# Seeding PSUM from ScalarE in a weight split, and a new order for the first ten units

## Chip, cores and metric

The kernel runs on one core of one Trainium2 chip. The metric is device microseconds of one execution; lower is better. Shown are the median of several runs and one profiled execution, whose span the trace covers instruction by instruction.

## What is computed

Three layers in fp32, on 3072 tokens (4 batches of 768), 8 heads of 48, so 384 features.

```python
for t in range(S):
    cur = einsum('bhd,bhe->bhde', u * k[t], v[t])
    y[t] = einsum('bhd,bhde->bhe', r[t], state + cur)
    state = w[t][..., None] * state + einsum('bhd,bhe->bhde', k[t], v[t])
...
h = x @ moe_w_in                       # 384 -> 1024
sm = softmax(h)
solu = h * sm
ln = (solu - mean(solu)) / sqrt(var(solu) + 1e-6) * g_ln
x = ln @ moe_w_out                     # 1024 -> 384
...
h = x @ moe2_w_in                      # 384 -> 2048
out = maximum(0.01 * h, h) @ moe2_w_out
```

The weights arrive as 64-bit floats. The kernel decodes them on the chip from pairs of 32-bit words into a high part and a low part (both fp32r, the form that TensorE multiplies in one pass), and computes each product as high by high, high by low and low by high.

## The kernel before

The tokens form 24 units of 128 rows (`NU`). A unit goes through the attention part (`prep…`, `att_…`), then `x_t`, `x_hi`, `x_lo` (turn it and split it), `mm1` (the 1024-wide product, 18 matmuls in two halves), the softmax steps (`soft_max`, `soft_e`, `soft_z`, `soft_nm`, `soft_c`, `soft_q`), `z_t`, `z_hi`, `z_lo` (turn and split again), and, three units at a time, `mm2` (the product with the output weights). The last layer (`mm3`, `g_…`, `mm4`) follows for the whole batch of tokens and fills more than half of the time with matmuls.

Nothing schedules itself: the order of work is three tables of step names, `FIRST` (units 0 to 9), `LOOP` (units 10 to 13) and `LAST`. Each entry calls a function, and each function appends its instructions to the queues of the engines, each of which runs its own queue strictly in that order. `warm` and `warm_k` are matmuls of constants whose result nobody reads.

The weights of the first layers are decoded in 14 slices, in the steps `w1_a` (ScalarE), `w1_e`, `w1_f`, `w1_h`, `w1_b` (VectorE), `w1_c` (split, ScalarE and TensorE) and `w1_d` (ScalarE). The first six slices ("i") are of `w_in`, 512 columns each; the other eight ("o") are of `w_out`, 384 columns each, and are multiplied by `g_ln` on the way. After `w1_b` the value stands as a tile `t` (the top of the number) and a negated rest in the low part's home (`w1ol` for "o"). `w1_c` must form t minus the negated rest minus the high part in PSUM (`PO`), for `w1_d` to copy out as the final low part. `ident` is an identity matrix in fp32, `minus` its negative in fp32r.

Of the kernel before, what the change touches and what calls it, by code (L numbers as in the profile page):

```python
# [43 lines left out]
0; att_mid 0; warm 13; w1_c; att_mul_next 0; prep_vd 0; w1_b; w1_d; att_y 0; att_state 0; prep4 1; load_g; att_x 0;
att_u 1; att_mid 1; w1_c; w1_b; prep_bonus 1; load_tr 2; w1_a; att_mul_next 1; prep_diag 1; load_tr 3; w1_d; prep1
2; att_scores 1; w1_e; x_t 0; load_nat 2; att_evac_s 1; load_o 1; prep2 2; w1_a; w1_c; x_hi 0; prep_vd 1; att_state
1; x_lm 0; x_lo 0; prep_k 2; w1_d; mm1 0 0; w1_f; att_kt 2; w1_a; prep3 2; mm1 0 1; prep_p 1; prep1 3; prep_check 2;
att_evac_k 2; prep_check 3; prep4 2; soft_max 0; att_y 1; prep_k 3; att_u 2; w1_a; w1_h; prep_p 2; att_x 1; att_mid
2; soft_e 0; warm_k 12; att_kt 3; warm_k 8; x_t 1; prep_bonus 2; att_scores 2; w1_e; att_evac_k 3; load_tr 4; soft_z
0; w1_g; w1_b; x_hi 1; prep_diag 2; prep_state 2; w1_f; x_lm 1; prep2 3; w1_c; att_evac_s 2; prep3 3; soft_nm 0;  # L50
x_lo 1; soft_c 0; mm1 1 0; w1_e; prep_p 3; prep_check 4; w1_h; w1_a; w1_f; w1_e; w1_h; prep_state 3; w1_b; w1_f;
w1_d; att_mul_next 2; z_t 0; prep4 3; w1_h; soft_q 0; load_nat 3; mm1 1 1; prep1 4; prep_vd 2; z_hi 0 0; z_lm 0 0;
w1_c; z_hi 0 1; prep_p 4; w1_b; z_lm 0 1; prep_k 4; z_lo 0 0; load_nat 4; att_scores 3; prep_bonus 3; z_lo 0 1;
w1_d; att_y 2; soft_max 1; att_x 2; w1_c; soft_e 1; w1_e; x_t 2; att_state 2; att_kt 4; x_hi 2; w1_a; soft_z 1;
prep_state 4; w1_f; prep2 4; soft_nm 1; w1_b; w1_h; w1_d; att_u 3; x_lm 2; w1_b; x_lo 2; w1_a; prep3 4; soft_c 1;
mm1 2 0; z_t 1; att_mid 3; w1_c; prep_diag 3; z_hi 1 0; load_tr 5; z_hi 1 1; att_mul_next 3; load_nat 5; z_lm 1 0;
att_evac_k 4; w1_e; att_state 3; att_evac_s 3; z_lm 1 1; w1_f; z_lo 1 0; prep1 5; prep_vd 3; mm1 2 1; w1_d; prep4 4;
att_u 4; z_lo 1 1; soft_q 1; att_y 3; soft_max 2; att_x 3; w1_h; prep_k 5; w1_c; att_mid 4; soft_e 2; prep_bonus 4;
x_t 3; w1_d; soft_z 2; w1_b; x_hi 3; att_kt 5; att_scores 4; prep_p 5; w1_e; x_lm 3; w1_c; prep_diag 4; w1_f; w1_a;
prep2 5; w1_e; x_lo 3; mm1 3 0; w1_h; soft_nm 2; prep_state 5; att_mul_next 4; att_evac_k 5; w1_b; w1_f; load_tr 6;  # L60
prep3 5; soft_c 2; w1_h; z_t 2; prep1 6; w1_d; prep_k 6; w1_c; z_hi 2 0; z_lm 2 0; prep_vd 4; mm1 3 1; z_hi 2 1;
w1_d; w1_b; z_lm 2 1; z_lo 2 0; att_state 4; att_evac_s 4; w1_c; soft_max 3; soft_q 2; z_lo 2 1; soft_e 3; att_y 4;
w1_d; att_u 5; prep4 5; att_x 4; soft_z 3; prep_check 5; att_scores 5; att_kt 6; prep_p 6; soft_nm 3; load_nat 6;
x_t 4; prep_bonus 5; prep2 6; x_hi 4; mm2a 4; soft_c 3; prep_check 6; soft_q 3; x_lo 4; load_tr 7; mm1 4 0; prep3 6;
prep4 6; prep_state 6; prep_bonus 6; z_t 3; z_hi 3 0; z_hi 3 1; att_mid 5; mm1 4 1; prep_diag 5; load_tr 8;
att_evac_k 6; z_lm 3 0; prep_vd 5; prep1 7; prep2 7; att_mul_next 5; att_evac_s 5; z_lo 3 0; z_lm 3 1; load_nat 7;
mm2b 4; att_scores 6; prep_p 7; soft_max 4; z_lo 3 1; mm2_out 4; prep_diag 6; att_state 5; prep3 7; att_y 5; att_u
6; prep_state 7; soft_e 4; mm2a 5; prep_check 7; att_x 5; soft_z 4; prep_k 7; prep4 7; x_t 5; mm2b 5; x_hi 5; x_lo
5; mm1 5 0; att_kt 7; soft_nm 4; prep_bonus 7; prep1 8; att_mid 6; soft_c 4; att_evac_s 6; att_mul_next 6; soft_q 4;
prep_vd 6; att_state 6; prep_k 8; mm2_out 5; z_t 4; prep_check 8; z_hi 4 0; z_hi 4 1; z_lo 4 0; z_lo 4 1; load_nat  # L70
8; prep2 8; mm1 5 1; att_evac_k 7; prep_diag 7; att_y 6; att_u 7; att_scores 7; soft_max 5; mm2a 6; att_x 6; att_kt
8; soft_e 5; prep_bonus 8; prep_p 8; x_t 6; att_mid 7; soft_z 5; soft_nm 5; prep3 8; prep_state 8; x_hi 6; prep_diag
8; soft_c 5; load_nat 9; load_tr 9; prep4 8; mm2b 6; x_lo 6; z_t 5; load_tr 10; prep_vd 7; att_mul_next 7; z_hi 5 0;
att_evac_s 7; z_hi 5 1; prep_bonus 9; att_state 7; prep_check 9; mm1 6 0; mm2_out 6; prep1 9; z_lo 5 0; att_evac_k
8; z_lo 5 1; prep_diag 9; mm1 6 1; soft_max 6; att_y 7; att_x 7; att_u 8; prep_p 9; soft_q 5; att_scores 8; prep1
10; soft_e 6; soft_z 6; mm2a 7; prep2 9; prep3 9; prep_vd 8; att_mid 8; att_mul_next 8; x_t 7; soft_nm 6; prep_k 9;
prep_k 10; mm2b 7; x_hi 7; x_lo 7; prep2 10; att_state 8; soft_c 6; mm1 7 0; z_t 6; mm2_out 7; att_evac_s 8; prep4
9; z_hi 6 0; prep_p 10; load_nat 10; z_hi 6 1; z_lo 6 0; mm1 7 1; att_kt 9; prep_state 9; z_lo 6 1; load_tr 11;
soft_max 7; soft_q 6; att_y 8; prep_vd 9; att_scores 9; prep_bonus 10; att_evac_k 9; att_u 9; att_x 8; soft_e 7;
att_kt 10; att_mid 9; soft_z 7; x_t 8; x_hi 8; soft_nm 7; att_mul_next 9; att_evac_s 9; att_evac_k 10; load_nat 11;  # L80
mm2a 8; x_lo 8; mm1 8 0; prep3 10; soft_c 7; z_t 7; prep1 11; prep_k 11; prep_diag 10; z_hi 7 0; prep_check 10; z_lo
7 0; att_state 9; soft_q 7; z_hi 7 1; prep_p 11; prep4 10; mm1 8 1; mm2b 8; prep_state 10; prep2 11; prep3 11;
prep_bonus 11; mm2_out 8; load_tr 12; z_lo 7 1; att_u 10; att_scores 10; prep_vd 10; soft_max 8; att_y 9; soft_e 8;
mm2a 9; att_x 9; prep_check 11; prep_state 11; x_t 9; mm2b 9; prep4 11; soft_z 8; att_mid 10; att_mul_next 10; x_hi
9; x_lo 9; prep1 12; soft_nm 8; prep_diag 11; soft_c 8; soft_q 8; att_evac_s 10; mm1 9 0; z_t 8; z_hi 8 0; prep_vd
11; load_tr 13; load_nat 12; mm2_out 9; mm1 9 1; prep_bonus 12; z_lo 8 0; prep_k 12; prep_p 12; att_state 10; z_hi 8
1; z_lo 8 1; prep2 12; prep_check 12; att_kt 11; att_evac_k 11
# [1086 lines left out]
```

## Time and profile before

| | |
|---|---|
| median of 3 runs | 740.12 us (739.97 to 740.4) |
| the profiled execution | 740.35 us, its span 738.6 us |
| TensorE, matmul | 721.6 us busy (98%) |
| VectorE | 502.4 us busy (68%) |
| ScalarE | 362.3 us busy (49%) |
| GpSimd | 193.9 us busy (26%) |

The shares are over the whole span, and the stages differ. In the first 340 us all the engines work on the attention part and the first layers; after that the time is almost only matmuls of the last layer. TensorE's records overlap, since a matmul is recorded until its last column has left the array: what one costs in a row of others is the distance between two starts, not its recorded length. For the other engines two records that follow each other without a wait overlap by some hundredths of a microsecond too.

### The profile page before, as it was taken

To read this page: it belongs to the slowest core of one execution; us is meant where nothing else is said; L and a number is where in the kernel's file an instruction comes from. 1 tells how busy PE (TensorE), PEld (TensorE's weight loads), DVE (VectorE), ACT (ScalarE), POOL (GpSimd) and SP (SyncE) were. 2 spreads that over 40 slices of the span, in tenths; PEclk is the share of its full clock that TensorE was granted. 3 is DMA by queue.
4 is the path that set the end of the run, shared out by engine and by line. 5 is a ranking of instruction groups with operands and counts; after the bars stand their busy time and mean duration, and the time that the engine had idled before them with its cause. 6 is when DMAs were issued, how large, how long until landed. Compare 5 with 4: busy or idle time off the path is not lost.

```text
span 738.6 us, 15199 instructions
## 1 busy us (share of the span) xinstructions
PE 721.6 (98%) x6243; PEld 607.4 (82%) x6243; DVE 502.4 (68%) x877; ACT 362.3 (49%) x668; POOL 193.9 (26%) x261
## 2 busy tenths in 40 slices
...
GB/s 327 280 168 109 130 149 115 140 151 102 184 149 166 117 110 77 79 120 159 190 130 86 43 65 1 92 80 0 1 86 0 1 12 32 1 1 43 1 0 47
DMA packets 30753, 69.10 MB, mean 94 GB/s; under 512 B 3260, under 2 KB 15956, under 8 KB 30548
## 3 DMA queue, kind: packets, MB, share of 16 engines
...
## 4 chain that ended last, share of the span: by engine, by line


## 5 line engine op out<-in xcount | busy, mean ns | idle before, releaser
L987 DVE TENSOR_TENSOR gw<-t,gh 128x512 fp32r<-128x512 f32 x96 | 68.2, 712 | 53.3 <-ACT gh L983 53.1
L983 ACT CAST gh<-t 128x512 fp32r<-128x512 f32 x96 | 59.2, 620 | 72.5 <-DVE t L979 58.3
L953 POOL TENSOR_TENSOR x2l<-x2l,x2h 128x1536 fp32r<-128x1536 f32 x4 | 14.1, 3514 | 276.8 <-ACT x2h L949 276.8
L979 DVE TENSOR_TENSOR t<-t,PZ 128x512 f32<-128x512 f32 x48 | 32.9, 686 | 68.7 <-ACT t L975 68.7
L979 DVE TENSOR_TENSOR t<-t,PK 128x512 f32<-128x512 f32 x48 | 32.9, 686 | 58.7 <-ACT t L975 58.7
L975 ACT ACTIVATE t<-PK 128x512 f32<-128x512 f32 x48 | 28.6, 596 | 73.8 <-PE PK L967 70.3
L975 ACT ACTIVATE t<-PZ 128x512 f32<-128x512 f32 x48 | 28.6, 596 | 71.8 <-PE PZ L967 71.0
L764 PE MATMUL PO<-zh,w1oh 128*128 128x384 f32 x168 | 59.9, 356 | 0.0
L708 PE MATMUL PH<-w1ih,xh 128*128 128x512 f32 x144 | 58.4, 405 | 0.1
L708 PE MATMUL PH<-w1ih,xl 128*128 128x512 f32 x144 | 57.0, 396 | 0.2
L708 PE MATMUL PH<-w1il,xh 128*128 128x512 f32 x144 | 56.4, 392 | 0.0
L764 PE MATMUL PO<-zh,w1ol 128*128 128x384 f32 x168 | 56.4, 336 | 0.0
L764 PE MATMUL PO<-zl,w1oh 128*128 128x384 f32 x168 | 56.3, 335 | 0.0
L967 PE MATMUL PK<-x2h,w2ih 128*128 128x512 f32 x144 | 56.2, 391 | 0.0
L967 PE MATMUL PZ<-x2h,w2ih 128*128 128x512 f32 x144 | 56.1, 390 | 0.0
L967 PE MATMUL PZ<-x2h,w2il 128*128 128x512 f32 x144 | 56.1, 389 | 0.0
L967 PE MATMUL PZ<-x2l,w2ih 128*128 128x512 f32 x144 | 56.1, 389 | 0.0
L967 PE MATMUL PK<-x2l,w2ih 128*128 128x512 f32 x144 | 56.0, 389 | 0.0
L967 PE MATMUL PK<-x2h,w2il 128*128 128x512 f32 x144 | 56.0, 389 | 0.0
L560 POOL TENSOR_TENSOR vd<-natv,dg 64x192 f32<-64x192 f32 (+1 forms) x57 | 36.5, 640 | 10.7 <-DVE dg L549 8.0
L997 PE MATMUL PH<-gw,w2oh 128*128 128x512 f32 x96 | 37.5, 390 | 0.5 <-DVE gw L987 0.5
L997 PE MATMUL PA<-gw,w2oh 128*128 128x512 f32 x96 | 37.4, 389 | 0.0
...
## 6 DMA issues: line engine op xcount, KB each, us to landing
...
```

Of the source, the lines that this page charges most:

```text
L560: pool.tensor_tensor(out=d[p:p + (64 if h else 128), h:h + 4], in0=nats[i][0][a, h:h + 4], in1=dgs[i][a, h:h + 4].to_broadcast([a.stop - a ...
L708: pe.matmul(out=PH[:, half], lhsT=a[:, kc], rhs=c[:, kc, 512 * half:512 * half + 512], start=(n == 0), stop=(n == 8))
L764: pe.matmul(out=o2[m], lhsT=a[:, c, 128 * m:128 * m + 128], rhs=d[:, c], start=(c == 0 and q == 0), stop=(c == K1 - 1 and q == 2))
L953: (dve if g < 2 else pool).tensor_tensor(out=xl, in0=f(xl), in1=f(xh), op=ALU.subtract)
L967: pe.matmul(out=h_at[n % 2], lhsT=a[:, kc, 128 * o:128 * o + 128], rhs=d[:, kc], start=(q == 0), stop=(q == 8))
L975: act.activation(out=gs[n][0], in_=h_at[n % 2], func=AF.Copy, scale=0.01)
L979: dve.tensor_tensor(out=t, in0=t, in1=h_at[n % 2], op=ALU.max)
L983: act.copy(out=gh, in_=t)
L987: dve.tensor_tensor(out=gw, in0=t, in1=f(gh), op=ALU.subtract)
L997: pe.matmul(out=at, lhsT=a[:, c % 4, 128 * o:128 * o + 128], rhs=d[:, a0:b0], start=(c == 0 and q == 0), stop=(c == K2 - 1 and q == 2 and ...
```

## The change

For the eight "o" slices, `w1_c` no longer scales `t` in place and copies it into PSUM by an identity product. ScalarE writes the scaled `t` straight into `PO`, makes the high part from `PO`, and TensorE only adds the two negative products onto what stands there. The six "i" slices stay as they were. The lines below are moved by four by the change (L856 of before is L860 for the "i" slices; for "o" the scaling is L854, the high part L855, the two products L856 and L857).

```diff
             key, t = w1_done.pop(0)
             hi, lo = w1_home(key)
+            d = PO[:, 0:t.shape[1]]
             if key[0] == "o":
-                act.activation(out=t, in_=t, func=AF.Copy, scale=gl[:, key[1]:key[1] + 1])
-            act.copy(out=hi, in_=t)
-            d = PO[:, 0:t.shape[1]]
-            pe.matmul(out=d, lhsT=ident, rhs=t, start=True, stop=False)
-            pe.matmul(out=d, lhsT=minus, rhs=lo, start=False, stop=False)
-            pe.matmul(out=d, lhsT=minus, rhs=hi, start=False, stop=True)
+                act.activation(out=d, in_=t, func=AF.Copy, scale=gl[:, key[1]:key[1] + 1])
+                act.copy(out=hi, in_=d)
+                pe.matmul(out=d, lhsT=minus, rhs=lo, start=False, stop=True, skip_group_check=True)
+                pe.matmul(out=d, lhsT=minus, rhs=hi, start=False, stop=True, skip_group_check=True)
+            else:
+                act.copy(out=hi, in_=t)
+                pe.matmul(out=d, lhsT=ident, rhs=t, start=True, stop=False)
+                pe.matmul(out=d, lhsT=minus, rhs=lo, start=False, stop=False)
+                pe.matmul(out=d, lhsT=minus, rhs=hi, start=False, stop=True)
             w1_low.append((lo, d))
```

The table `FIRST` is another one; `LOOP` and `LAST` are the same. It holds the same steps but for the warming: 34 matmuls of `warm` in place of 45, and 8 of `warm_k` in place of 20. Its beginning, before and now:

```diff
-load_w 1; w1_a; prep1 0; prep_check 0; w1_e; prep2 0; load_w 2; load_w 3; prep_state 0; w1_a; w1_a; w1_f; prep_k 0;
-w1_h; prep3 0; att_kt 0; w1_b; load_tr 1; prep4 0; w1_c; w1_e; w1_e; prep_p 0; prep_state 1; load_nat 0; w1_f;
+load_w 1; prep_state 0; w1_a; prep_p 0; prep1 0; load_w 2; w1_e; prep_check 0; prep2 0; w1_a; w1_a; load_w 3; w1_f;
+prep3 0; w1_a; w1_h; prep_k 0; prep4 0; load_tr 1; w1_b; w1_e; w1_e; w1_c; w1_f; w1_a; w1_f; w1_d; w1_h; load_nat 0;
...
```

TensorE at the second "o" slice, right behind the second half of unit 1's `mm1` (L708). L683 subtracts a high part of `z` in PSUM, L583 are the scores and L647 and L654 the outputs of the attention. Before:

```order
242 L708 MATMUL PH<-w1ih,xl 128x512
243 L683 MATMUL PZ_99<-zh,minus 128x512
244 L856 MATMUL PO<-w2s,ident 128x384
245 L857 MATMUL PO<-w1ol,minus 128x384
246 L858 MATMUL PO<-w1oh,minus 128x384
247 L683 MATMUL PZ_100<-zh,minus 128x512
248 L583 MATMUL PA<-lt,kt 64x64 x16
249 L647 MATMUL PZ_99<-natv,ss_121 64x48 x16
```

and now:

```order
195 L708 MATMUL PH<-w1ih,xl 128x512
196 L683 MATMUL PZ_99<-zh,minus 128x512
197 L856 MATMUL PO<-w1ol,minus 128x384
198 L857 MATMUL PO<-w1oh,minus 128x384
199 L683 MATMUL PZ_100<-zh,minus 128x512
200 L647 MATMUL PZ_99<-natv,ss_121 64x48 x16
```

The identity product is gone, the place of the slice is the same, and the scores of the next unit have moved behind the attention outputs.

ScalarE at the same slice, from the square of unit 0 (L731) and the high part of `z` (L747) to the low parts of `z` (L752). L864 and L868 are `w1_d`, L486 is `prep_check`. Before:

```order
53 L731 ACTIVATE ebuf,q_all<-zbuf 128x1024
54 L747 CAST zh<-PZ_99 128x4x128
55 L853 ACTIVATE w2s<-w2s,gl 128x384
56 L854 CAST w1oh<-w2s 128x384
57 L747 CAST zh<-PZ_100 128x4x128
58 L752 CAST zl<-PZ_99 128x4x128
59 L752 CAST zl<-PZ_100 128x4x128
60 L864 CAST w1ol<-PO 128x384
```

and now:

```order
50 L731 ACTIVATE ebuf,q_all<-zbuf 128x1024
51 L747 CAST zh<-PZ_99 128x4x128
52 L486 ACTIVATE junk,flags<-tr,blo 112x512
53 L486 ACTIVATE junk,flags<-tr,bhi 112x512
54 L854 ACTIVATE PO<-w2s,gl 128x384
55 L855 CAST w1oh<-PO 128x384
56 L747 CAST zh<-PZ_100 128x4x128
57 L752 CAST zl<-PZ_99 128x4x128
58 L868 CAST w1ol<-PO 128x384
59 L752 CAST zl<-PZ_100 128x4x128
```

The scaling writes `PO`, the high part reads it, and a check of a later unit's decay factors stands ahead of both.

VectorE from the first scan of unit 0 on (L492, L517 and L526 are `prep1`, `prep3` and `prep4`, L503 is `prep_k`; L825, L827, L830 and L832 are the four steps of a weight slice). Before:

```order
8 L827 SCALAR_TENSOR_TENSOR ebuf<-zh,ebuf 128x512
9 L503 TENSOR_TENSOR kt<-tr,suf 112x512
10 L830 TENSOR_SCALAR zh<-ebuf 128x512
11 L517 SCALAR_TENSOR_TENSOR e_168<-tr,e_112 112x520
12 L832 SCALAR_TENSOR_TENSOR w1il<-zh 128x512
13 L526 TENSOR_TENSOR lt<-tr,e_168 112x512
```

and now:

```order
8 L827 SCALAR_TENSOR_TENSOR ebuf<-zh,ebuf 128x512
9 L517 SCALAR_TENSOR_TENSOR e_165<-tr,e_112 112x520
10 L830 TENSOR_SCALAR zh<-ebuf 128x512
11 L503 TENSOR_TENSOR kt<-tr,suf 112x512
12 L526 TENSOR_TENSOR lt<-tr,e_165 112x512
13 L832 SCALAR_TENSOR_TENSOR w1il<-zh 128x512
```

The same six instructions stand in another order, with the last step of the first weight slice behind both products of unit 0.

## Rows read from the trace of the kernel before

**Rows 1.** Stages: us of each engine busy (instructions), granted clock, DMA share, GB/s.

```profile
core 0: us, PE busy (x) PEld busy (x) DVE busy (x) ACT busy (x) POOL busy (x), PEclk, DMA share, GB/s
4.00:38.00 34.00, 28.61 (x291) 17.99 (x293) 31.09 (x50) 20.70 (x45) 12.38 (x10) 1.00 0.84 323
38.00:76.00 38.00, 37.63 (x493) 29.34 (x489) 35.91 (x67) 34.52 (x70) 18.98 (x25) 1.00 0.40 127
76.00:220.00 144.00, 143.29 (x2196) 128.13 (x2196) 126.29 (x214) 88.16 (x172) 91.62 (x132) 1.00 0.44 141
320.00:450.00 130.00, 129.49 (x601) 109.00 (x600) 106.98 (x218) 67.60 (x122) 7.91 (x3) 1.00 0.33 104
```

**Rows 2.** Waits of TensorE, whole span: us in total, times, longest us.

```profile
PE PK L576 <- DVE kt L503: 9.1, 1, 9.1
PE PH L997 <- DVE gw L987: 0.5, 1, 0.5
```

**Rows 3.** Timeline of TensorE, seventh "o" slice: start us, recorded us, instruction.

```profile
71.32 0.81 PE L856 MATMUL PO<-w2s,ident 128*128 128x384 f32 x2
71.67 0.63 PE L857 MATMUL PO<-w1ol,minus 128*128 128x384 f32 x1
72.14 0.34 PE L858 MATMUL PO<-w1oh,minus 128*128 128x384 f32 x1
72.32 0.39 PE L683 MATMUL PZ<-zh,minus 128*128 128x512 f32 x1
```

**Rows 4.** Timeline of ScalarE, high parts of "o" slices 1 and 7.

```profile
42.40 0.51 ACT L854 CAST w1oh<-w2s 128x384 fp32r<-128x384 f32 x1
...
70.82 0.51 ACT L854 CAST w1oh<-w2s 128x384 fp32r<-128x384 f32 x1
```

**Rows 5.** Timeline of TensorE, identity product of "o" slice 1.

```profile
42.42 0.91 PE L856 MATMUL PO<-w2s,ident 128*128 128x384 f32 x2
```

**Rows 6.** Groups of ScalarE, 38 to 90 us: busy us, mean ns | idle before.

```profile
L853 ACT ACTIVATE w2s<-w2s,gl 128x384 f32<-128x384 f32 x8 | 5.0, 628 | 0.0
...
L854 ACT CAST w1oh<-w2s 128x384 fp32r<-128x384 f32 x8 | 4.1, 513 | 0.3
...
L693 ACT CAST xh<-PZ 128x384 fp32r<-128x384 f32 x4 | 1.9, 484 | 1.0 <-PE PZ L675 1.0
```

**Rows 7.** Waits of ScalarE, 40 to 78 us (all there are).

```profile
ACT w1ol L864 <- PE PO L858: 0.9, 2, 0.6
ACT xh L693 <- PE PZ L675: 0.6, 1, 0.6
ACT ebuf L716 <- DVE nmax L713: 0.3, 1, 0.3
```

**Rows 8.** Waits of VectorE, 38 to 76 us (all but one of 0.2).

```profile
DVE x L662 <- PE PZ L654: 0.8, 1, 0.8
DVE x L662 <- ACT w1oh L854: 0.7, 1, 0.7
DVE nmax L713 <- PE PH L708: 0.3, 1, 0.3
```

**Rows 9.** Waits of VectorE, 76 to 220 us, the longest two.

```profile
DVE nmax L713 <- PE PH L708: 5.7, 7, 1.6
DVE zl L754 <- ACT zh L747: 5.6, 7, 1.8
```

**Rows 10.** Groups of TensorE, whole span: matmuls of constants from `warm`.

```profile
L567 PE MATMUL PH<-zero 128*128 128x384 bf16 x45 | 8.7, 346 | 0.0
```

**Rows 11.** Timeline of VectorE, the row maximum of unit 3.

```profile
75.02 1.21 DVE L713 TENSOR_REDUCE nmax<-PH 128x1 f32<-128x1024 f32 x1
```

**Rows 12.** Every `prep4` product on VectorE: duration ns min/median/max, first and last start.

```profile
L526 DVE TENSOR_TENSOR lt<-tr,e x24: 647/787/1985, 10.9 to 292.7; 112x512 f32<-112x512 f32 x24
```

**Rows 13.** Timelines of VectorE and GpSimd around the longest of them.

```profile
26.58 1.99 DVE L526 TENSOR_TENSOR lt<-tr,e 112x512 f32<-112x512 f32 x1
...
27.02 0.99 POOL L544 TENSOR_TENSOR natq<-natq 128x384 f32<-128x384 f32 x1
28.09 1.33 POOL L545 TENSOR_TENSOR natq<-natq,ub 128x384 f32<-128x384 f32 x1
```

More of the change, by code (lines that the diff above doesn't have):

```diff
@@ L44 @@
[L44 to L87, printed above, removed]
+load_w 1; prep_state 0; w1_a; prep_p 0; prep1 0; load_w 2; w1_e; prep_check 0; prep2 0; w1_a; w1_a; load_w 3; w1_f;
@@ new lines @@
+prep3 0; w1_a; w1_h; prep_k 0; prep4 0; load_tr 1; w1_b; w1_e; w1_e; w1_c; w1_f; w1_a; w1_f; w1_d; w1_h; load_nat 0;
+att_kt 0; w1_e; w1_b; w1_a; warm 11; w1_c; w1_h; w1_f; w1_b; w1_e; w1_h; w1_f; load_tr 2; w1_b; prep_p 1; w1_d;
+prep1 1; warm 4; w1_c; att_evac_k 0; prep2 1; w1_e; load_u; w1_d; warm 4; w1_c; w1_h; att_u 0; prep_k 1; w1_f;
+att_kt 1; w1_d; att_scores 0; prep_bonus 0; w1_b; w1_c; prep3 1; prep_diag 0; att_mid 0; w1_h; att_mul_next 0;
+prep_vd 0; att_state 0; att_evac_k 1; prep_check 1; att_evac_s 0; load_nat 1; prep4 1; prep_check 2; warm 15; att_y
@@ new lines @@
+0; att_x 0; att_u 1; att_mid 1; prep_bonus 1; prep1 2; load_o 0; prep_k 2; att_scores 1; w1_b; x_t 0; load_nat 2;
+prep_state 1; prep2 2; load_g; w1_d; w1_c; prep_diag 1; w1_a; x_hi 0; w1_e; prep3 2; load_tr 3; w1_a; att_evac_s 1;
+load_o 1; att_mul_next 1; att_state 1; prep4 2; prep_vd 1; x_lm 0; prep1 3; w1_a; prep_state 2; prep_state 3; warm_k
+8; att_kt 2; w1_f; x_lo 0; mm1 0 0; w1_d; prep_check 3; mm1 0 1; prep_k 3; att_evac_k 2; soft_max 0; att_y 1; att_u
+2; w1_a; prep_p 2; prep_bonus 2; w1_h; att_kt 3; att_x 1; w1_g; soft_e 0; att_mid 2; att_evac_k 3; w1_e; soft_z 0;
@@ new lines @@
+x_t 1; att_scores 2; load_tr 4; x_hi 1; x_lm 1; soft_nm 0; w1_b; w1_f; prep_diag 2; w1_c; w1_e; prep2 3; x_lo 1; mm1
+1 0; soft_c 0; w1_a; att_evac_s 2; w1_d; w1_h; w1_e; z_t 0; w1_f; soft_q 0; prep3 3; load_nat 3; z_hi 0 0; w1_h;
+prep_check 4; att_mul_next 2; w1_b; mm1 1 1; z_lm 0 0; w1_f; w1_c; w1_e; load_nat 4; z_hi 0 1; w1_b; prep1 4; z_lo 0
+0; z_lm 0 1; prep_vd 2; w1_d; z_lo 0 1; prep4 3; att_y 2; att_scores 3; load_tr 5; prep_k 4; prep_p 3; w1_c;
+soft_max 1; att_x 2; att_kt 4; prep_bonus 3; soft_e 1; x_t 2; w1_h; w1_a; att_state 2; x_hi 2; soft_z 1; w1_b; att_u
@@ new lines @@
+3; w1_a; prep2 4; x_lm 2; prep_state 4; w1_d; x_lo 2; w1_e; soft_nm 1; soft_c 1; w1_f; mm1 2 0; att_mid 3;
+att_evac_k 4; w1_f; z_t 1; w1_h; w1_c; prep_diag 3; z_hi 1 0; w1_a; z_lm 1 0; z_hi 1 1; w1_h; att_mul_next 3;
+att_state 3; z_lo 1 0; w1_d; soft_q 1; att_evac_s 3; prep3 4; mm1 2 1; prep1 5; z_lm 1 1; z_lo 1 1; w1_b; soft_max
+2; att_y 3; att_u 4; prep4 4; prep_vd 3; w1_c; att_x 3; soft_e 2; att_mid 4; soft_z 2; prep_k 5; w1_b; x_t 3; w1_e;
+w1_f; w1_d; x_hi 3; att_scores 4; x_lm 3; att_kt 5; w1_h; w1_c; w1_e; prep_bonus 4; x_lo 3; att_evac_s 4;
@@ new lines @@
+att_mul_next 4; mm1 3 0; soft_nm 2; att_state 4; w1_b; w1_f; soft_c 2; w1_d; load_nat 5; w1_h; att_evac_k 5; z_t 2;
+prep_p 4; prep2 5; w1_c; prep3 5; z_hi 2 0; z_lm 2 0; w1_b; z_hi 2 1; prep_diag 4; mm1 3 1; z_lm 2 1; prep4 5; z_lo
+2 0; soft_q 2; load_tr 6; w1_d; prep_vd 4; z_lo 2 1; att_y 4; soft_max 3; att_u 5; w1_c; att_scores 5; att_x 4;
+w1_d; prep1 6; load_nat 6; prep_p 5; soft_e 3; prep_k 6; prep_p 6; x_t 4; x_hi 4; soft_z 3; x_lo 4; soft_nm 3; mm2a
+4; soft_c 3; prep2 6; mm1 4 0; prep_state 5; z_t 3; mm1 4 1; prep_check 5; z_hi 3 0; att_evac_s 5; prep_check 6;
@@ new lines @@
+att_mid 5; att_kt 6; z_lm 3 0; att_mul_next 5; load_tr 7; prep3 6; z_hi 3 1; soft_q 3; prep4 6; z_lm 3 1; prep_bonus
+5; soft_max 4; mm2b 4; att_scores 6; z_lo 3 0; z_lo 3 1; prep_diag 5; load_tr 8; soft_e 4; prep1 7; att_evac_k 6;
+att_state 5; att_y 5; prep_bonus 6; prep_vd 5; soft_z 4; soft_nm 4; prep_diag 6; mm2_out 4; att_u 6; mm2a 5;
+load_nat 7; prep_state 6; prep_k 7; att_x 5; att_mid 6; prep2 7; x_t 5; att_mul_next 6; x_hi 5; soft_c 4; x_lo 5;
+prep_check 7; prep1 8; mm2b 5; att_state 6; prep3 7; prep4 7; mm1 5 0; z_t 4; z_hi 4 0; prep_vd 6; att_kt 7;
@@ new lines @@
+att_evac_k 7; z_lo 4 0; mm2_out 5; prep_bonus 7; z_hi 4 1; prep_p 7; prep_check 8; prep_p 8; mm1 5 1; att_evac_s 6;
+att_u 7; prep_state 7; load_tr 9; z_lo 4 1; soft_q 4; att_y 6; soft_max 5; att_scores 7; att_mid 7; mm2a 6;
+prep_state 8; prep2 8; prep_k 8; att_x 6; x_t 6; soft_e 5; soft_z 5; soft_nm 5; mm2b 6; x_hi 6; x_lo 6; soft_c 5;
+prep3 8; mm1 6 0; z_t 5; att_mul_next 7; z_hi 5 0; att_kt 8; att_evac_s 7; prep4 8; load_nat 8; prep1 9; z_lo 5 0;
+prep_diag 7; mm1 6 1; prep_k 9; prep_vd 7; prep_bonus 8; z_hi 5 1; att_evac_k 8; z_lo 5 1; soft_q 5; load_tr 10;
@@ new lines @@
+mm2_out 6; att_state 7; soft_max 6; att_y 7; prep_check 9; soft_e 6; att_x 7; soft_z 6; soft_nm 6; att_u 8;
+att_scores 8; att_kt 9; att_evac_k 9; x_t 7; att_mid 8; x_hi 7; mm2a 7; x_lo 7; att_mul_next 8; soft_c 6; load_nat
+9; mm1 7 0; prep2 9; prep3 9; att_evac_s 8; prep_diag 8; prep_bonus 9; z_t 6; mm2b 7; mm1 7 1; prep1 10; prep_vd 8;
+att_state 8; soft_q 6; mm2_out 7; z_hi 6 0; prep4 9; z_hi 6 1; z_lo 6 0; att_scores 9; prep_diag 9; att_u 9; z_lo 6
+1; prep_p 9; att_y 8; prep2 10; soft_max 7; att_x 8; load_tr 11; soft_e 7; prep_state 9; prep3 10; mm2a 8; soft_z 7;
```

11 lines of the change are left out of this document (8 added, 3 removed).

## Prediction

> **What bounds the kernel now.** I read first the busy time by stage [rows 1], then TensorE's list of waits [rows 2], then the timelines of single engines where the change sits. In the stages TensorE is busy 37.63 of 38 us, 143.29 of 144 and 129.49 of 130, and apart from the 9.1 us before its first product the longest entry in its list of waits is 0.5 us [rows 2]. So TensorE is the bound of the whole, and work taken from it in the first 76 us arrives at the end, unless another engine steps in. The candidates stand in the same table: between 38 and 76 us VectorE is busy 35.91 of 38 us and ScalarE 34.52 [rows 1], with few waits (1.8 us in the three rows of VectorE, and 1.8 us for ScalarE over 40 to 78 us) [rows 7, 8]. This is the stage in which the eight "o" slices are split. Three engines are nearly full there at once, so what a shorter TensorE is worth hangs on the waits of the other two.
>
> **The identity product.** In the seventh slice the three products start at 71.32, 71.67 and 72.14 us, and the next matmul at 72.32 [rows 3]. The whole takes 1.00 us, and the last subtraction alone 72.32 - 72.14 = 0.18. Two subtractions stay (0.36), so the identity product costs 0.64 us of TensorE's time, and the eight of them 5.1 us. In that stage TensorE hardly waits, so all of it is on its path.
>
> **A wait that the change adds.** The low-part subtraction now changes `PO` while ScalarE makes the high part from it, so it has to stand behind that cast; before, only the last of the three products did. I compare TensorE's start of each slice with the end of the cast. Slice 1: 42.40 + 0.51 = 42.91 against a start at 42.42 [rows 4, 5], so 0.49 us would be waited. Slice 7: 70.82 + 0.51 = 71.33 against 71.32 [rows 3, 4], 0.01. Six of the eight slices would wait, the first and the seventh being these; the six come to 0.49, 0.49, 0.11, 0.10, 0.35 and 0.01, in sum 1.55 us. Behind the waiting instruction stand the following matmuls of TensorE's queue, the whole stream. The bounds: nothing, if the new order puts other matmuls ahead of the slice, and 8 x 0.51 = 4.1 us, if TensorE is always there as soon as the scaling ends. In the order of the second slice its neighbours are the same as before, so I take the value of the old arrivals, 1.55.
>
> **ScalarE.** The high part is now cast from PSUM: a cast of the same size from PSUM took 484 ns (L693) against 513 ns from SBUF (L854) [rows 6], so 8 x 0.03 = 0.2 us less, all of it in the wait just counted. The scaling took 628 ns from SBUF to SBUF [rows 6]; writing PSUM from ScalarE is not in this trace. I bound it by the 484 ns of the shortest operation of that size and, to the other side, by as much above 628 as that is below, 772 ns: 8 x 0.144 = 1.2 us either way. I take 628, the same operation on the same elements, thus no change.
>
> The Trainium skill, page "Perfetto Trace Analysis", section "Optimizing Scalar/DVE Operations", puts ScalarE's fixed cost at about 93 ns on SBUF and 51 ns on PSUM. By it the scaling would be an estimated 42 ns shorter, 0.3 us in eight, and the sum as much lower. No run here shows a write to PSUM by ScalarE yet.
>
> **Warming and moves.** Eleven matmuls of `warm` and twelve of `warm_k` go. One of `warm` is recorded with 346 ns [rows 10], so the eleven are at most 3.8 us; I count nothing, since they fill TensorE's time up to 38 us, where VectorE sets the pace (31.09 us busy of 34, and TensorE 28.61 with those matmuls in it [rows 1]). If the cover were gone, that is if TensorE were the bound there, up to 3.8 us more would be gained; if the granted clock, 1.00 in these rows (2.4 GHz), came later for it, TensorE would lose time where it has some. All steps other than these keep their instructions, so VectorE, GpSimd and the queue of SP have the same work. In SP's queue the third transposed load now stands ahead of the second unit's natural one; the DMA share up to 38 us is 0.84 [rows 1], so there is some room, and I count nothing for it. A displaced load would show as a wait of GpSimd's bonus products.
>
> **The sum.** -5.1 (identity) + 1.55 (new wait) - 0.2 (shorter cast) = -3.75 us. Against the profiled execution's 740.35 us that is 736.6; the median of the runs shown lies 0.2 lower, so I forecast 736.5 for the median of the changed kernel. With all the ends: -5.1 - 0.2 - 1.2 = -6.5, or -5.1 + 4.1 + 1.2 = +0.2, thus 733.9 to 740.6.
>
> Does it arrive? Up to 76 us VectorE's waits leave some 1.8 us [rows 8] and those of ScalarE as much [rows 7], so about half of the 3.75 can be had by then, with the maximum of unit 3 at some 73.2 instead of 75.02 [rows 11]. TensorE is then a further 1.9 us ahead of VectorE, and VectorE's 5.7 us of waits for `mm1` between 76 and 220 us [rows 9] shrink by that. After 320 us TensorE has no waits to lose it to.
>
> **Rivals.** *VectorE takes the gain.* Only its waits that TensorE releases shrink before 76 us, 0.8 + 0.3 = 1.1 us [rows 8], and those for `mm1` later [rows 9] turn out to be the delay of a unit's own chain (attention, turn, split, `mm1`), which doesn't shorten. Then 739.2. For it speaks VectorE's share, against it that its waits for `mm1` come seven times, with up to 1.6 us.
>
> *Slower: GpSimd's products meet VectorE's.* The same `prep4` product takes 647 ns at best and 1985 at worst [rows 12], and the longest ran while GpSimd multiplied `natq` twice [rows 13]. One such meeting costs 1.34 us on VectorE, which has next to no waits before 76 us to absorb it. The new order shifts both engines against each other. From the third additional meeting on (4.0 us) the 3.75 are used up; five would give 740.35 - 3.75 + 6.7 = 743.3. Against it: the old order had such meetings too, and as many may vanish. The Trainium skill, page "SBUF — State Buffer", section "Who interferes with whom", says that a VectorE instruction with two SBUF inputs contends with a GpSimd instruction that reads SBUF, since they share a port pair. By that rule every such pair of the new order that overlaps costs one of the two engines; the trace agrees, 1985 ns against 647.
>
> *The order gives more.* If the new places hide the added wait (0) and half of the 5.7 us for `mm1` goes, it is -5.1 - 2.9 = -8.0, so 732.4. For it speaks that the waits in [rows 8, 9] are there to be had; against it that a unit's chain has its own length.
>
> That the change does not do what it says is no case: the order shows the eight identity products gone.
>
> **Chances.** A measurement of this kernel can tell about 0.2%, 1.5 us, from no change. The forecast (734.5 to 738.6) has 0.52, the larger gain 0.14, VectorE as the bound 0.20, the meetings 0.14. The first two are faster; of the third a tenth too, the rest is within 0.2%; the last is slower: 0.68, 0.18, 0.14. The range 733.5 to 742.0 takes in the forecast, VectorE's case and the nearer halves of the other two, and leaves out some 0.15.
>
> **What would show it.** Right: TensorE's list has the two subtractions of an "o" slice 0.18 us apart, with waits for L855's cast of at most 0.5 us on some; the maximum of unit 3 starts near 73; VectorE's waits for `mm1` after 76 us fall below 4 us; the stages after 340 us keep their lengths. Wrong: waits for the cast that sum to over 3 us; the maximum of unit 3 at 75 or later, with `prep4` or the scans longer in the mean (meetings) or with TensorE waiting for VectorE (its bound); or a scaling far from 628 ns.

## The result, and the profile after

The changed kernel takes **746.21 us** (median of 6 runs, 745.03 to 748.83) against 740.14 for the kernel before in the same job: ratio 1.0085 [1.0069, 1.0102], 6 us slower where 736.5 was forecast. The profiled execution took 745.03 us, with a span of 743.3.

The stages, with columns as in [rows 1] (the third, 76 to 220 us, is left out):

```profile
4.00:38.00 34.00, 27.59 (x270) 16.38 (x271) 28.39 (x46) 20.84 (x45) 11.00 (x9) 1.00 0.86 324
38.00:76.00 38.00, 33.96 (x454) 26.68 (x452) 34.68 (x66) 29.90 (x62) 16.40 (x19) 0.91 0.33 111
...
320.00:450.00 130.00, 129.42 (x601) 108.65 (x600) 106.28 (x218) 68.96 (x124) 8.33 (x4) 1.00 0.36 111
```

From 320 us on next to nothing differs. The loss lies in the first two rows: VectorE did 2.7 us less work by 38 us (28.39 against 31.09), and between 38 and 76 us the granted clock is 0.91 where it was 1.00. How it builds up is read from the starts of the same instructions in both traces (us):

| start of | before | after | later by |
|---|---|---|---|
| `mm1` of unit 0 | 32.61 | 35.26 | 2.66 |
| `mm1` of unit 1 | 43.52 | 46.70 | 3.18 |
| `mm1` of unit 2 | 55.59 | 60.56 | 4.98 |
| maximum of unit 3 [rows 11] | 75.02 | 79.21 | 4.18 |
| `mm1` of unit 10 | 159.26 | 163.70 | 4.44 |
| first of `mm3` | 327.23 | 332.31 | 5.08 |
| end of the trace | 738.56 | 743.31 | 4.75 |

Two steps make it, at two places. **The first: before 30 us.** The timeline of TensorE of the changed kernel (start us, recorded us, instruction; in brackets the idle time before it and what ended it):

```profile
26.72 2.61 PE L567 MATMUL PH<-zero 128*128 128x384 bf16 x15
29.26 0.96 PE L647 MATMUL PZ<-natv,ss 64*64 64x48 f32 x26
...
43.65 0.55 PE L675 MATMUL PZ<-ident,x 128*128 128x128 f32 x3 [1.43 <-DVE x L665]
...
45.92 0.66 PE L856 MATMUL PO<-w1ol,minus 128*128 128x384 f32 x1 [0.64 <-DVE w1ol L832]
...
46.70 0.63 PE L708 MATMUL PH<-w1ih,xh 128*128 128x512 f32 x1
47.13 0.63 PE L708 MATMUL PH<-w1il,xh 128*128 128x512 f32 x1
...
75.97 0.42 PE L856 MATMUL PO<-w1ol,minus 128*128 128x384 f32 x1
76.23 0.33 PE L857 MATMUL PO<-w1oh,minus 128*128 128x384 f32 x1
```

and that of VectorE at the same time:

```profile
27.26 1.37 DVE L526 TENSOR_TENSOR lt<-tr,e 112x512 f32<-112x512 f32 x1
30.97 0.56 DVE L662 TENSOR_TENSOR x<-PZ,vd 128x384 f32<-128x384 f32 x1 [2.35 <-PE PZ L654]
31.95 1.24 DVE L492 TENSOR_TENSOR_SCAN suf<-tr,sel 112x520 f32<-112x520 f32 x1
```

Fifteen matmuls of `warm` (L567) take TensorE from 26.72 to 29.26; behind them in its queue stands unit 0's attention output (L647, L654), and VectorE waits 2.35 us for it (L662), with the next scan behind. That is nearly the 2.66 us of the table. (At the same place the kernel before has no such wait: its L662 starts at 28.49.)

**The second: 42 to 52 us.** TensorE idles for 1.43 us up to 43.65, waiting for VectorE's `x` (L665), and for 0.64 up to 45.92, waiting for VectorE's low part of the first "o" slice (L832). The granted clock then falls. The windows of the changed kernel, columns as above:

```profile
43.00:44.00 1.00, 0.35 (x3) 0.31 (x3) 0.92 (x3) 0.54 (x2) 0.92 (x2) 1.00 0.92 350
44.00:45.00 1.00, 1.00 (x35) 0.74 (x33) 0.99 (x1) 0.77 (x2) 0.08 (x1) 0.99 0.20 66
45.00:46.00 1.00, 0.36 (x2) 0.11 (x1) 1.00 (x4) 0.97 (x4) 0.67 (x2) 0.50 0.00 0
...
50.00:51.00 1.00, 1.00 (x5) 0.70 (x5) 1.00 (x4) 0.00 (x0) 0.00 (x0) 0.50 0.00 0
51.00:52.00 1.00, 1.00 (x8) 1.00 (x6) 1.00 (x4) 0.37 (x1) 0.00 (x0) 0.59 0.00 0
```

The kernel before, at the same place:

```profile
42.00:44.00 2.00, 1.93 (x8) 1.31 (x9) 2.00 (x7) 1.97 (x4) 1.58 (x3) 1.00 0.33 117
44.00:46.00 2.00, 2.00 (x12) 1.67 (x11) 2.00 (x4) 1.97 (x6) 0.48 (x1) 1.00 0.82 261
```

From 45 to nearly 52 us the clock is 0.50 (1.2 GHz), and the first half of unit 1's `mm1` steps by 0.43 us a matmul (46.70, 47.13) instead of 0.23. In the kernel before, TensorE was busy for 3.93 us between 42 and 46 us, and the clock stayed at 1.00 (2.4 GHz).

The new instructions themselves did nearly what was forecast. The rows by line (ns: min/median/max):

```profile
L854 ACT ACTIVATE PO<-w2s,gl x8: 566/592/635, 44.6 to 79.8; 128x384 f32<-128x384 f32 x8
L855 ACT CAST w1oh<-PO x8: 478/478/480, 45.2 to 80.4; 128x384 fp32r<-128x384 f32 x8
```

and of TensorE's waits in the whole span:

```profile
PE PO L856 <- ACT w1oh L855: 0.7, 3, 0.3
PE PO L856 <- DVE w1ol L832: 0.6, 1, 0.6
```

The scaling into PSUM takes 592 ns (628 into SBUF [rows 6]), the cast out of PSUM 478 (513). Two subtractions of a slice start 0.26 us apart (75.97, 76.23), not 0.18. So the loss is not in the new code, and the experiments take the two halves of the change apart.

### The profile page after: what moved, and what is told of

The parts are those of the page before. It is cut to its first block, busy times and chain, and to the rows that moved or that the text cites. A ratio compares the mean times of both kernels' runs of the same rounds, so it can differ in the third digit from the quotient of the medians.

```text
span 743.3 us, 15141 instructions
## 1 busy us (share of the span) xinstructions
PE 721.5 (97%) x6204; PEld 605.3 (81%) x6204; DVE 502.4 (68%) x877; ACT 361.6 (49%) x668; POOL 193.7 (26%) x261
## 4 chain that ended last, share of the span: by engine, by line
## 5 line engine op out<-in xcount | busy, mean ns | idle before, releaser
L708 PE MATMUL PH<-w1ih,xh 128*128 128x512 f32 x144 | 59.1, 410 | 0.1
L708 PE MATMUL PH<-w1ih,xl 128*128 128x512 f32 x144 | 57.4, 398 | 0.1
L708 PE MATMUL PH<-w1il,xh 128*128 128x512 f32 x144 | 57.2, 397 | 0.0
L1001 PE MATMUL PA<-gh,w2oh 128*128 128x512 f32 x96 | 37.4, 389 | 0.0
```

The costliest lines, as they stand in the source:

```text
L708: pe.matmul(out=PH[:, half], lhsT=a[:, kc], rhs=c[:, kc, 512 * half:512 * half + 512], start=(n == 0), stop=(n == 8))
L1001: pe.matmul(out=at, lhsT=a[:, c % 4, 128 * o:128 * o + 128], rhs=d[:, a0:b0], start=(c == 0 and q == 0), stop=(c == K2 - 1 and q == 2 and ...
```

## The experiments

**Code and order apart.** The first (e1) has the new `w1_c` with the table of before, the second (e2) the new table with the old `w1_c`. Put in words, against the kernel before:

```diff
-(w1_c as before)                # e1
+(w1_c as changed)
-(FIRST as before)               # e2
+(FIRST as changed)
```

> The order of before with the new split of the eight output-weight slices. Theory A (the loss lies in the new order: warm matmuls on TensorE's path before 30 us and a stretch of half clock from 45 to 52 us; the split itself saves what the prediction worked out): about 736.5 us, 3 to 5 us below before, granted clock 0.999, no low stretch near 45 us. Rival B (the write to PSUM and the wait for the cast cost more than the identity product): 742 us or more. Rival C (VectorE sets the pace of the stage): 739 to 740 us.

Measured: 739.39 us (738.73 to 741.24), ratio 0.9992 [0.9983, 1.0001].

> The new order with the old split (identity product for all 14 slices). Theory A: slower than the changed kernel by what the identity products are worth, 748 to 750 us, with the same low clock around 45 us. Rival B: below the changed kernel, 741 to 744 us. Rival C: the same as the changed kernel within 1 us.

Measured: 745.1 us (744.57 to 746.62), ratio 1.0069 [1.0055, 1.0083]. Its clock rows show the same fall, for a shorter time:

```profile
42.00:44.00 2.00, 0.61 (x10) 0.45 (x14) 1.90 (x5) 1.31 (x5) 1.66 (x3) 0.99 0.92 357
44.00:46.00 2.00, 2.00 (x34) 1.58 (x34) 2.00 (x5) 1.87 (x5) 0.93 (x2) 0.50 0.01 4
46.00:48.00 2.00, 2.00 (x7) 1.60 (x6) 2.00 (x7) 2.00 (x5) 1.23 (x2) 0.66 0.23 35
```

So the order alone costs about 5 us, and the code alone gives under 1; both miss what the first theory expected (736.5, and 748 to 750). The two ratios multiply to 1.0061, and the changed kernel has 1.0085 [1.0069, 1.0102]. The clock goes with this: averaged over a whole execution it is 0.992 to 0.994 in all six of the changed kernel and 0.996 in all five of e2, as in the traces, where it is low for 6.8 and for 3.4 us. Why it is low for longer in the changed kernel is not shown; between 44 and 46 us its TensorE was busy for 1.36 us, that of e2 for 2.00.

**The order's two faults.** Into the changed kernel, warming matmuls were put where TensorE idled (e3); the fifteen on the path were taken out (e4); both (e5); and both with the first warming moved to the start (e6):

```diff
-warm 15; att_y 0                                  # e4, e5, e6
+att_y 0
-att_kt 3; att_x 1; ... prep_diag 2; w1_c          # e3, e5, e6
+att_kt 3; warm_k 36; att_x 1; ... prep_diag 2; warm_k 14; w1_c
-prep_state 0; w1_a; ... warm 11; ... warm 4; ... warm 4    # e6
+prep_state 0; warm 20; w1_a; ... warm 5
```

> The changed kernel with 36 small constant matmuls behind the turn of unit 3's keys and 14 ahead of the first output-weight slice, where TensorE idles at 42 to 46 us. Theory A: the granted clock stays at 1.00 there, the first half of unit 1's mm1 takes 2.1 us and not 3.8, and the time falls by about 2 us, to 744. Rival C (VectorE is late anyway): the clock stays up and the time does not change by more than 0.5 us.

> The changed kernel without the 15 constant matmuls ahead of unit 0's attention outputs. Theory A: att_y of unit 0 starts about 1.9 us earlier (27.4 instead of 29.26), VectorE's wait of 2.3 us for it falls to 0.5, and the time falls by 1.5 to 2 us, to 744.3, if the clock is not lost there. Rival C: VectorE's wait turns into another and the time stays within 0.5 us. If the clock falls at 27 us for lack of work: slower than the changed kernel.

> The changed kernel with both edits: no 15 constant matmuls ahead of unit 0's attention outputs, and 36 + 14 small ones where TensorE idled at 42 to 46 us. Theory A (those two are the loss): the granted clock stays at 1.00 once it has risen, and the time is 740.2 us or less (741.4 of the run without the 15, less some 1.2 us that the half clock took from unit 1's mm1). Rival (the rest of the new order is worse by itself): 741 us or more.

> As the kernel with both edits, with 20 constant matmuls at the very start, 5 instead of 11 ahead of the second weight slice and none where 4 + 4 stood. Theory A: the clock rises before the first product (about 6 us instead of 16), unit 0's mm1 starts at 31.5 to 32.5 us instead of 32.7, and the time is 0 to 1 us below the kernel with both edits. Rival (VectorE, busy without a wait from 6 us on, sets the start of unit 0's mm1): no change beyond 0.3 us. If the clock falls again for lack of matmuls: slower by 1 us or more.

Measured, with the starts as differences to the kernel before (us):

| | median | ratio | `mm1` 0 | `mm1` 2 | max 3 | `mm3` |
|---|---|---|---|---|---|---|
| changed kernel | 746.21 | 1.0085 [1.0069, 1.0102] | +2.66 | +4.98 | +4.18 | +5.08 |
| e3, idle time filled | 742.32 | 1.0029 [1.0018, 1.0039] | +2.05 | +2.34 | +1.55 | +1.79 |
| e4, without the fifteen | 741.39 | 1.0026 [1.0012, 1.0039] | +0.10 | +1.31 | +0.51 | +0.72 |
| e5, both | 740.73 | 1.0007 [0.9998, 1.0016] | +0.07 | +0.33 | -0.47 | -0.20 |
| e6, warmed at the start | 739.92 | 1.0002 [0.9994, 1.0011] | +0.25 | +0.51 | -0.27 | -0.17 |

The differences are from one trace each. In e4 `mm1` of unit 0 is back in its place, since VectorE's wait is 0.5 us; timeline of VectorE in e4:

```profile
28.42 0.56 DVE L662 TENSOR_TENSOR x<-PZ,vd 128x384 f32<-128x384 f32 x1 [0.50 <-PE PZ L654]
```

but up to `mm1` of unit 2 another 1.2 us is lost, since the clock still falls (0.50 from 44 to 46 us). It doesn't fall in all of e4's eleven executions: the three with a mean clock of 0.999 take 740.4 to 740.7 us, and the four with 0.991 to 0.994 take 743.4 to 744.3, so its median stands between two groups and a long fall alone costs some 3.5 us there. In e3 the reverse: unit 0 stays late, and between 42 and 46 us the filling holds the clock at 1.00; windows of e3:

```profile
42.00:44.00 2.00, 1.61 (x57) 1.32 (x54) 1.90 (x5) 1.40 (x5) 1.40 (x2) 1.00 0.74 283
44.00:46.00 2.00, 1.71 (x35) 1.40 (x28) 2.00 (x5) 1.97 (x5) 1.27 (x2) 1.00 0.03 5
```

With both, the mean clock is 0.999 or more in all eleven executions, and e5 is level with the kernel before: 5.5 of the 6 us are back. The two faults are nearly all of the loss, but not all of it. Against e1, which has the same code in the old order, e5 is still some 1.1 us behind (ratios 1.0007 and 0.9992). What in the new order costs that stays open. The gains of e3 and e4 (3.9 and 4.8 us) sum to more than the 5.5 of e5, so they overlap: in seven of e4's eleven executions the mean clock is 0.995 or more, in none of the changed kernel's six. The clock before 18 us has no part in the loss: in e6 the clock is high first and low later, by the windows of e6,

```profile
4.00:10.00 6.00, 3.07 (x15) 1.28 (x12) 4.02 (x7) 2.29 (x5) 0.00 (x0) 1.00 0.97 349
11.00:17.00 6.00, 4.35 (x12) 2.65 (x13) 5.89 (x13) 4.38 (x8) 0.00 (x0) 0.50 1.02 411
```

and unit 0's `mm1` moves by only 0.2 us against e5. Where no block of warming stands in its way, VectorE (5.89 of those 6 us) sets the start, as the prediction had it.

**Where the 5.1 us of the identity products stayed.** e1 has no fault of order, and gains 0.9 us. Its row for the second stage:

```profile
38.00:76.00 38.00, 34.62 (x507) 27.24 (x504) 36.06 (x67) 34.18 (x70) 18.99 (x25) 1.00 0.39 128
```

and its timeline of TensorE at slices 1, 2, 3, 5 and 6 and what follows them:

```profile
43.02 0.41 PE L856 MATMUL PO<-w1ol,minus 128*128 128x384 f32 x1 [0.64 <-ACT w1oh L855]
43.27 0.34 PE L857 MATMUL PO<-w1oh,minus 128*128 128x384 f32 x1
...
49.26 0.45 PE L856 MATMUL PO<-w1ol,minus 128*128 128x384 f32 x1 [0.41 <-ACT w1oh L855]
49.55 0.34 PE L857 MATMUL PO<-w1oh,minus 128*128 128x384 f32 x1
...
53.47 0.55 PE L675 MATMUL PZ<-ident,x 128*128 128x128 f32 x3 [0.43 <-DVE x L665]
...
64.43 0.34 PE L857 MATMUL PO<-w1oh,minus 128*128 128x384 f32 x1
65.43 0.55 PE L675 MATMUL PZ<-ident,x 128*128 128x128 f32 x3 [0.67 <-DVE x L665]
...
67.98 0.42 PE L856 MATMUL PO<-w1ol,minus 128*128 128x384 f32 x1 [0.62 <-ACT w2s L814]
```

TensorE is busy 34.62 us instead of 37.63: 3.0 of the 5.1 us that were freed became idle. At slices 1 and 2 the identity product had run while ScalarE made the high part; without it TensorE waits there for that cast (0.64 and 0.41), and the last subtraction starts 0.08 and 0.19 us sooner (43.35 and 49.74 before). Behind slices 3 and 5 it is sooner by 0.50 and 0.69 us, and TensorE then waits 0.43 and 0.67 for the `x` of VectorE. At slice 6 the identity product had run while VectorE made the low part (L832, which ends at 67.88 before and at 67.83 in e1); without it TensorE waits 0.62 us (the profile names another instruction, of ScalarE), and the last subtraction starts no sooner (68.23, against 68.21). The maximum of unit 3 starts at 74.98, against 75.02.

Which of the others holds it? First, two runs with less VectorE work, on the kernel before (e7) and on e1 (e8):

```diff
-            dve.tensor_reduce(out=dg, in_=nats[i][1][:, 0], axis=AX.X, op=ALU.add)
+            part = nats[i][1][:, 0, :, 0:2] if 2 <= i <= 4 else nats[i][1][:, 0]
+            dve.tensor_reduce(out=dg, in_=part, axis=AX.X, op=ALU.add)
...
-                dve.tensor_scalar(out=top, in0=t, ...)
+                m = 512 if key[0] == "i" else 192
+                dve.tensor_scalar(out=top[:, 0:m], in0=t[:, 0:m], ...)
```

> The kernel before with less work on VectorE between 38 and 76 us: the sums of the diagonal (L549) of units 2 to 4 go over 2 of 48 elements, and the third decode step (L830) of the eight output-weight slices over 192 of 384 columns, about 2.7 us less by the recorded lengths. Leaves out that part of the sums and of the masking. Theory V (VectorE alone sets the pace there): 2 to 2.7 us faster, 737.6 to 738.3. Theory P (TensorE alone sets it, as predicted): no change beyond 0.5 us. Theory VP (each is at its limit and takes what the other gives): 0.3 to 1.2 us faster.

Measured: 740.63 us, 1.0007 [0.9998, 1.0016].

> The old order with the new split, and the same lighter VectorE work; leaves out the same part of the sums and of the masking. Theory V: 2 to 2.7 us below the run with the split alone (739.4), thus 736.7 to 737.4, and as far below before_light as that split alone was below before (0.9). Theory P: no change against 739.4. Theory VP: with both lightened the gain is more than the sum of the single ones, 736 to 737.5, while each alone gave about 1.

Measured: 738.95 us, 0.9985 [0.9976, 0.9994]. Neither tells the theories apart, since the edit did not make VectorE lighter on the whole: it was busy 35.84 us in e7 against 35.91 between 38 and 76 us. The single operations did become shorter: the three sums take 163 ns in place of 543 (medians), and six of the eight masks some 250 in place of 350. But the other two masks take 648 and 714 (782 and 364 in the kernel before), and the shift of the same slices (L826 here) 561 in the mean in place of 359; the longest of them ran while GpSimd multiplied and took 0.35 us at the same place in the kernel before. Rows of e7:

```profile
L832 DVE TENSOR_SCALAR zl<-w2s x4: 239/252/714, 56.6 to 72.4; 128x192 int32<-128x192 int32 x4
...
58.69 1.33 DVE L826 TENSOR_SCALAR w2s<-w2s 128x384 int32<-128x384 int32 x1
...
58.98 0.82 POOL L557 TENSOR_TENSOR vd<-natv,dg 128x384 f32<-128x384 f32 x1
```

The next four go by other operations. e9 doubles the identity product of the kernel before; e10 and e11 lighten one engine in e1, and e12 both. e10 and e12 leave out half of the variance sums of four units and most of one range check; e11 and e12 take the maximum of four units over half of the columns:

```diff
+            if key[0] == "o":                                                    # e9
+                pe.matmul(out=d, lhsT=ident, rhs=t, start=True, stop=True)
             pe.matmul(out=d, lhsT=ident, rhs=t, start=True, stop=False)
...
-            act.activation(out=ebuf, in_=zbuf, func=AF.Square, ...)              # e10, e12
+            m = 512 if i < 4 else F1
+            act.activation(out=ebuf[:, 0:m], in_=zbuf[:, 0:m], func=AF.Square, ...)
...
+            m = 1 if i == 4 else 8                                               # e10, e12
...
-                act.activation(out=junk[0:112], in_=wr, ...)
+                act.activation(out=junk[0:112, 0:m], in_=wr[:, 0:m], ...)
...
-            dve.tensor_reduce(out=nmax[:, i:i + 1], in_=flat(PH), ...)           # e11, e12
+            m = 512 if i < 4 else F1
+            dve.tensor_reduce(out=nmax[:, i:i + 1], in_=flat(PH)[:, 512:512 + m] if i < 4 else flat(PH), ...)
```

> The kernel before with the identity product of each output-weight slice issued twice (the second overwrites the first): 8 x 0.64 = 5.1 us more on TensorE. P (TensorE paces the stage 38 to 76 us, as the prediction said): close to +5.1 us, so about 745, with the maximum of unit 3 some 4 us later than 75.02. S or V (ScalarE or VectorE paces it and TensorE is only nearly full): part of it goes into TensorE's waits, of which there are about 2 us up to 76 us, so at least +1 and at most +3.5 us: 741 to 743.5. If adding 5.1 costs much more than removing 5.1 gave (0.9), TensorE stands at the edge between being the bound and not being it.

> The kernel before with the new code of the split in the old order (739.39 earlier), and ScalarE lightened: the squares for the variance of units 0 to 3 over 512 of 1024 columns, one range check over 1 of 8 chunks, some 2.5 us less on ScalarE by 76 us (part of the variance sums and of the range check is left out). S (ScalarE paces 38 to 76 us once the identity products are gone): the missing gain appears, maximum of unit 3 near 72.5, time 736.8 to 738. V (VectorE paces): no change, 739 to 739.8. A unit's chain through several engines paces it: under 1 us, 738.5 to 739.2.

> The same split in the old order, and VectorE lightened: the row maxima of units 0 to 3 are taken over 512 of 1024 columns from PSUM, 4 x some 0.55 = 2.2 us less (the softmax is shifted by another value, which cancels). V: maximum of unit 3 near 73, time 737 to 738. S: no change, 739 to 739.8. A unit's chain through several engines, in which the maximum is a link: the next exponential starts 0.55 us sooner in each unit, and a gain appears in part, 738 to 739.

> Both lightenings together with the new split in the old order. S: as with ScalarE alone, V: as with VectorE alone. If both run level, so that neither alone gives much: clearly more than the sum of the two alone, 736 to 737.5. P (TensorE paces): none of the three changes anything, 739 to 739.8.

| | median | ratio | `mm1` 1 | `mm1` 2 | max 3 | `mm1` 4 | `mm3` |
|---|---|---|---|---|---|---|---|
| e9, identity twice | 743.87 | 1.0051 [1.0038, 1.0065] | +0.65 | +1.23 | +3.53 | +4.38 | +3.91 |
| e1, new code alone | 739.39 | 0.9992 [0.9983, 1.0001] | -0.07 | +0.01 | -0.04 | -0.81 | -1.14 |
| e10, ScalarE lighter | 739.13 | 0.9994 [0.9985, 1.0003] | -0.19 | -0.11 | -0.16 | -0.92 | -1.40 |
| e11, VectorE lighter | 739.16 | 0.9991 [0.9982, 1.0] | -0.12 | -0.02 | -0.07 | -0.82 | -1.33 |
| e12, both lighter | 738.19 | 0.9977 [0.9967, 0.9986] | -0.16 | -1.07 | -1.00 | -1.76 | -2.28 |

Adding 5.1 us of TensorE's work costs 3.8 us, removing them gives 0.9: TensorE stands just at the edge. In e9 the 0.64 us of the first slice is still swallowed (it shows at `mm1` of unit 1 and is gone at unit 1's maximum, 50.60 against 50.62), and the others are paid nearly in full; there the other two wait for TensorE (VectorE's work in 50 to 56 us falls to 4.07 us, from 5.18 before):

```profile
50.00:56.00 6.00, 6.00 (x103) 4.61 (x105) 4.07 (x8) 3.71 (x8) 3.84 (x4) 1.00 0.32 126
```

Each lightening took about 2 us off its engine between 38 and 76 us (ScalarE 32.24 in e10 and VectorE 34.29 in e11, against 34.18 and 36.06 in e1). Neither alone adds to what e1 has (0.9994 and 0.9991 against 0.9992). Both together take a further 0.15%, about 1.1 us; the intervals of e12 and e1 still touch, and the traces show the same 1.1 us at `mm3`. Unit 1's maximum (the reduction of `nmax`) and the `x` behind it show how. Timelines of VectorE (line numbers are moved by one to three by the edits), in e10 (ScalarE lighter):

```profile
50.52 1.21 DVE L714 TENSOR_REDUCE nmax<-PH 128x1 f32<-128x1024 f32 x1
51.66 0.54 DVE L663 TENSOR_TENSOR x<-PZ,vd 128x384 f32<-128x384 f32 x1
...
52.69 1.20 DVE L827 TENSOR_SCALAR w2s<-w2s 128x384 int32<-128x384 int32 x1
53.92 0.36 DVE L633 TENSOR_TENSOR st<-PA,ao 112x192 f32<-112x192 f32 x1
```

in e11 (VectorE lighter):

```profile
50.58 0.70 DVE L714 TENSOR_REDUCE nmax<-PH 128x1 f32<-128x512 f32 x1
52.33 0.56 DVE L662 TENSOR_TENSOR x<-PZ,vd 128x384 f32<-128x384 f32 x1 [1.05 <-ACT w1oh L856]
```

and in e12 (both):

```profile
50.57 0.67 DVE L715 TENSOR_REDUCE nmax<-PH 128x1 f32<-128x512 f32 x1
51.51 0.56 DVE L663 TENSOR_TENSOR x<-PZ,vd 128x384 f32<-128x384 f32 x1 [0.27 <-ACT w1oh L858]
...
63.38 0.56 DVE L663 TENSOR_TENSOR x<-PZ,vd 128x384 f32<-128x384 f32 x1 [1.32 <-ACT ebuf L718]
```

In e11 VectorE is done 0.5 us sooner and waits the longer, 1.05 us, behind ScalarE's queue (by the profile for the high part of the next slice); `x` stays where it was. In e10 that wait is gone and `x` starts 0.7 us sooner, right behind the maximum; but a shift behind it (L827) takes 1.20 us in place of 0.56 (in e1), while GpSimd multiplies (52.68 to 53.68), and the instruction after that starts at 53.92 as before (54.03). With both, `x` is 0.9 us sooner, and that arrives. At unit 2 it does not: there the shorter maximum only lengthens the wait for `x` (1.32 us), whose attention outputs stand behind `mm1` on a TensorE that is busy from 56 to 62 us without a gap. So each of the three engines sets the pace somewhere in these 38 us.

## Why the prediction was wrong

**The mechanism of the slices was right, and its price too.** The identity product costs what it was put at: with a second one, the last subtraction of slice 1 starts 0.64 us later (43.99 in e9, against 43.35), and 3.8 to 4.4 of the 5.1 us for eight arrive in the time. The added wait for the cast was put at 1.55 us and is 1.2 in e1, 0.7 in the changed kernel. The sum left out the 0.62 us at slice 6, where the identity product had stood in a wait for VectorE, and took the subtractions at 0.18 us each; the first of a slice takes 0.25 to 0.29 in seven of e1's eight. Both new ScalarE operations are shorter by 34 to 36 ns in the medians; 0.2 us had been counted for the cast and nothing for the scaling.

The Trainium skill's rule that the sum had set aside, page "Perfetto Trace Analysis", section "Optimizing Scalar/DVE Operations" (by its figures ScalarE's fixed cost is an estimated 42 ns less on PSUM), is borne out in sign and nearly in size, by the 36 ns of the scaling. It would not have moved the forecast by more than 0.3 us.

**The step that failed first: warming and moves counted at nothing.** "They fill TensorE's time up to 38 us, where VectorE sets the pace" looked at the sum that goes away and not at where the rest lands. VectorE does set the pace (e6), but it also waits for TensorE at one point, the attention output of unit 0, and the fifteen matmuls now stand right ahead of that: VectorE waits 2.35 us, and unit 0's `mm1` is 2.1 to 2.7 us late (e3, e2, changed kernel). The new table shows it, in a `warm 15` directly ahead of `att_y 0`.

The other part is the clock. The prediction named, in half a sentence, a clock that comes later, counted nothing, and had none that falls in the middle. Between 42 and 46 us TensorE was busy for 1.93 us of 4 (0.57 and 1.36 in the two halves), the clock fell to 1.2 GHz, and the first half of unit 1's `mm1` ran at half speed. At this place the table took away more than the twelve of `warm_k`: all twenty stood around `att_kt 3`, and the eight that stay now stand ahead of `att_kt 2`. TensorE of the kernel before:

```profile
39.52 0.52 PE L571 MATMUL PK<-zero 128*128 128x64 bf16 x12
39.88 0.58 PE L576 MATMUL PK<-ident,kt 112*128 112x112 f32 x4
40.30 0.40 PE L571 MATMUL PK<-zero 128*128 128x64 bf16 x8
40.58 0.55 PE L675 MATMUL PZ<-ident,x 128*128 128x128 f32 x3
```

By the starts, the twenty took 0.64 us there, and TensorE then went on with next to no wait. In the changed kernel it idles for 2.07 us at the same steps. So the missing warming is a third of the gap at most, and the rest is TensorE waiting for VectorE in the new order, the moves of the same term. e3 and e5 show that filling the gap removes the fall, with 50 matmuls; that the twenty would have done is not shown.

The clock also came later at the start, as the prediction had feared, and that cost nothing. The granted clock of 1.00 over 4 to 38 us [rows 1] hides a low stretch: the first `warm` matmuls step by 0.32 us in the changed kernel (eleven from 13.95 to 17.47), and later ones by 0.17 (fifteen from 26.72 to 29.26). Before, eighteen step by 0.20 in the mean (12.56 to 16.17), so the rise came sooner. Yet unit 0's `mm1` is in its place in e4 and e5 (+0.10 and +0.07).

The Trainium skill, page "TensorE: Matmul & The Clock Gate", section "Part 1: The HAM clock gate", says that the slow clock is the default and that activity lifts it. The trace agrees (1.00 with TensorE busy 3.93 of 4 us, 0.50 behind the idle time).

**The step that failed second: "TensorE is the bound of the whole".** A busy share of 37.63 of 38 us says that adding work costs, which e9 confirms. It doesn't say that removing work gives: VectorE and ScalarE were nearly as full, and the prediction saw that, but still let half of the gain through by 76 us and the rest later. In e1 nothing had come by 76 us (the maximum of unit 3 at 74.98, with TensorE waiting for VectorE, is one of the prediction's own signs of being wrong); 0.8 us came at `mm1` of unit 4, and 0.3 to 0.5 after it. What came is near the case "VectorE takes the gain" (739.2 against 739.39 for e1), but that is luck in part: VectorE alone is not the taker (e11).

**The rivals.** Slower was forecast by meetings of GpSimd and VectorE. The size came near (743.3), the mechanism is another: the longest `prep4` product in the changed kernel takes 1791 ns against 1985, and e5, with the same order of VectorE and GpSimd, is level with the kernel before. VectorE's waits for `mm1` in the units up to 220 us didn't fall below 4 us but stayed at 5.4 (5.7 before [rows 9], 5.8 in e1).

No version beats the kernel before by more than its interval without leaving work out: the new code in the old order is the nearest, at 0.9992 [0.9983, 1.0001]. Not tried was a new fit of the order with both faults forbidden, and ScalarE's casts of the slices moved ahead in its queue, where e12 says a gain would start.
